# Moving the two magnitude products of the kernel tables from VectorE to GpSimd, and a longer wait for the tables' matmuls

## The chip, the cores and the metric

The kernel runs on one core of one Trainium2 chip. The metric is device time in microseconds (us) from one launch of the whole kernel. Engines are called PE (TensorE, the matmuls; PEld is its loading of weights), DVE (VectorE), ACT (ScalarE), POOL (GpSimd, which also issues some of the transfers) and SP (which issues most of the others).

## The reference

The input `x` is 2048 tokens by 576 channels, float32. It is normalised, and the result goes two ways: through a long convolution along the tokens (S4D: the convolution kernel of each channel is a sum over 128 complex exponentials), and through a two-layer MLP over the channels with 4608 hidden units.

```python
xn = layernorm(x)
# S4D: kernel K (576 x 2048), convolution by FFT
dt = exp(log_dt); A = -exp(log_A_real) + 1j*A_imag; C = (C_real + 1j*C_imag)*dt[:, None]
P = exp((A*dt[:, None])[:, :, None] * pos)          # 576 x 128 x 2048
K = 2*einsum("dn,dnl->dl", C, P).real
s = irfft(rfft(xn.T, 2L) * rfft(K, 2L))[:, :L].T + xn*D_skip
# MLP, gated
h = gelu(layernorm(xn) @ w1 + b1)
g = silu(h @ w2 + b2)
out = x + s*g
```

## The kernel before

**MLP.** The MLP sets the length of the kernel. Its products are made with operands split into a high and a low part, three matmuls for each product. Tokens are taken in 4 blocks of 512, hidden units in 12 groups of 3 x 128. One *pass* (a "slot" in the code; there are 48) is one group with one block: three times 14 matmuls of the first layer (L519, into the PSUM tiles `mxa` and `mxb`), then 72 matmuls of the second layer (L585). Between the two layers, for each of the three parts of 128 hidden units: ACT makes `h` (gelu, L552), ACT makes its high half `hh` (L555), DVE makes the low half `hl` as `h - hh` (L558). The third `hl` of a pass is needed by the 21st matmul of the second layer. DVE also adds the second layer's results into `acc` (L595) and makes the low halves of the weights (`w1l`, `w2l`, L496).

**Tables.** The convolution kernel is built from 36 tables, one for 16 channels each (`tables(b)`). The parameters `par` are loaded from memory (L810, issued by POOL, two buffers). A table's work is split into steps: phases and sines (DVE L828, L831, L837; ACT), the magnitudes `mg` (`mags`, L853: two products of broadcast parameters, of 1024 and 512 elements a partition; one buffer), and four products of sines and magnitudes (`weigh`, L864, L866, L868, L870) that give `U` and `v`. PE then makes 64 small matmuls from `U` and `v` (`kgen`, L910), which give a piece of the convolution kernel. The products `weigh` of the next table wait for these matmuls, since `U` and `v` have one buffer.

**Convolution.** Six chunks of 96 channels each go through transform steps on PE (L982, L1021, L1074, L1106), with DVE and ACT work between them. These steps use the PSUM tile `cv`.

**Order.** Each engine works through its instructions in the order in which the program is written, and a planner (class `Order`) decides that order when the kernel is built. Every step has an engine and an expected duration, for instance `dve(n)`, `act(n)` or `pool(n)` for n elements; the planner keeps a clock for each engine, sorts the steps of several *lines* into the stream, and holds back a DVE or ACT step that would delay a piece of the MLP that is due. The cost functions are

```python
def dve(n):
    return 0.075 + 0.00104 * n
...
def pool(n):
    return 0.25 + 0.0023 * n
```

The small PE steps (tables and convolution) are placed between the MLP's matmuls by `pe_turns`. A table's matmuls can go in two ways. They *ride*: when a convolution step is placed and the table is ready, `ride` puts the table's 64 matmuls at the head of that step. Or they go *alone*, but once the convolution has started only when the table has been ready for `ALONE` microseconds of planned PE time:

```python
if x is kl and pace["started"] and kl["steps"][0]["mark"][1] < NB - 1 and od.t["PE"] < h[1] + ALONE:
    break
```

Of the kernel before, what the change touches and what calls it, by code (L numbers as in the profile page):

```python
# [42 lines left out]
def dve(n):  # L43
    return 0.075 + 0.00104 * n


def act(n):
    return 0.06 + 0.00098 * n


def pool(n):
    return 0.25 + 0.0023 * n
# [155 lines left out]
def step(eng, dur, fn, need=(), mark=None, cv=0, at=0.0, late=0.0, tbl=None, by=1e9):  # L208
    return dict(eng=eng, dur=dur, fn=fn, need=tuple(need), mark=mark, cv=cv, at=at, late=late, tbl=tbl, by=by)
# [3 lines left out]
def mixer_kernel(ctx, tc, u, log_a_real, a_imag, c_real, c_imag, log_dt, d_skip, w1, b1, w2, b2,  # L213
                 f1, f2, g2, g1, tvals, ident, out, parts=("mlp", "s4d")):
    nc = tc.nc
# [589 lines left out]
    def load_par(b):  # L805
        if b == NB:
            return
        PAR[b] = sb.tile([P, SB, NPAR], F32, name="par", bufs=2)

        nc.gpsimd.dma_start(PAR[b].rearrange("p (g i) k -> p g (i k)", g=4), dram(  # L810
            par_s, (b // 6 * CH + b % 6 * 4) * NPAR, [[D * NPAR, P], [24 * NPAR, 4], [1, 4 * NPAR]]))

    def bc(ap, dim, n):

        a = [list(x) for x in ap.ap]
        a.insert(dim, [0, n])
        return bass.AP(tensor=ap.tensor, offset=ap.offset, ap=a)

    def tables(b):

        T = {}

        def phase(k):
            if k == 0:
                T["w"] = sb.tile([P, 2, SB, NV], F32, name="w", bufs=2)
                nc.vector.tensor_mul(T["w"][:, 1], bc(PAR[b][:, :, 0], 2, NV), bc(tv, 1, SB))  # L828
            else:
                u = T["w"][:, 1, :, 32:]  # L830
                nc.vector.tensor_add(u, u, bc(PAR[b][:, :, 1], 2, 32))  # L831

        def whole():
            nc.scalar.activation(T["w"][:, 0].bitcast(I32), T["w"][:, 1], AF.Copy)

        def frac():
            nc.vector.tensor_sub(T["w"][:, 1], T["w"][:, 1], T["w"][:, 0].bitcast(I32))  # L837

        def fold():
            nc.scalar.activation(T["w"][:, 0], T["w"][:, 1], AF.Abs)  # L840

        def sin(k):
            w = T["w"][:, k]
            if k == 0:
                nc.scalar.activation(w, w, AF.Sin, bias=halfpi[:, 0:1], scale=-TWO_PI)
            else:
                nc.scalar.activation(w, w, AF.Sin, scale=TWO_PI)

        def mags(k):
            if k == 0:  # L850
                T["m"] = sb.tile([P, SB, NM], F32, name="mg")
            n, e1, e8 = ((8, E1, E8), (4, E32, E256))[k]
            nc.vector.tensor_mul(T["m"][:, :, 64 * k:64 * k + 8 * n].rearrange("p c (i j) -> p c i j", i=n),  # L853
                                 bc(PAR[b][:, :, e8:e8 + n], 3, 8), bc(PAR[b][:, :, e1:e1 + 8], 2, n))

        def weigh(k, part):

            if part == 0:
                T["v"] = sb.tile([P, 2, SB, 64], F32, name="v")
                T["U"] = sb.tile([P, 2, SB, 32], F32, name="U")  # L860
                TAB[b] = (T["U"], T["v"])
            w, v, m = T["w"], T["v"], T["m"]
            if part == 0:
                nc.vector.tensor_mul(T["U"], w[:, :, :, 32:], bc(m[:, :, 64:], 1, 2))  # L864
            elif part == 1:
                nc.vector.tensor_mul(v[:, :, :, :32], w[:, :, :, :32], bc(m[:, :, :32], 1, 2))  # L866
            elif k == 0:
                nc.vector.tensor_mul(v[:, k, :, 32:], w[:, k, :, 31::-1], m[:, :, 32:64])  # L868
            else:
                nc.vector.scalar_tensor_tensor(v[:, k, :, 32:], w[:, k, :, 31::-1], -1.0, m[:, :, 32:64],  # L870
                                               op0=OP.mult, op1=OP.mult)

        n = SB * 32
        f = lambda g, *a: lambda: g(*a)
        return ([step(None, 6.0 if b < 3 else 4.5, lambda: load_par(b), mark=("par", b), need=[("pack", ((b // 6 + 1) * CH - 1) // PK)]
                      + ([("mags", b - 2)] if b > 1 else [("xn", k) for k in range(8, NT)])),
                 step("DVE", dve(SB * NV), f(phase, 0), need=[("wu", b - 2, 1)] if b > 1 else []),
                 step("DVE", dve(n), f(phase, 1)), step("ACT", act(SB * NV), whole),
                 step("DVE", dve(SB * NV), frac), step("ACT", act(SB * NV), fold, mark=("fold", b))],
                [step("ACT", act(SB * NV), f(sin, 0), need=[("fold", b)], mark=("sin", b, 0), tbl="sin"),  # L880
                 step("ACT", act(SB * NV), f(sin, 1), mark=("sin", b, 1), tbl="sin")],
                [step("DVE", dve(2 * n), f(mags, 0), need=[("par", b)]),
                 step("DVE", dve(n), f(mags, 1), mark=("mags", b))]
                + [step("DVE", dve(2 * n) if part < 2 else dve(n), f(weigh, k, part),
                        need=[("sin", b, int(part < 2))] + ([("kg", b - 1)] if b else []),
                        mark=("wu", b, 1) if k else None) for k, part in ((0, 0), (0, 1), (0, 2), (1, 2))])
# [491 lines left out]
    def wmark(n, which):  # L1378

        per = KB + 1 + G  # L1380
        a = n * per + (0 if which == 1 else KB + 1)
        return [("w", k) for k in range(a, a + (KB + 1 if which == 1 else G))]
# [21 lines left out]
    for k in range(4):  # L1404
        gl["steps"].append(step("POOL", 5.0, lambda k=k: part.update({k: load_g2(k)}), mark=("g2", k),
                                need=[("g2c", k - 1)] if k else []))
# [10 lines left out]
    def table_lines():  # L1417
        for b in range(NB):
            for x, y in zip((tl, sl, vl), tables(b)):
                x["steps"] += y  # L1420
            kl["steps"] += kgen(b)
# [21 lines left out]

    pace = dict(left=NCH * (2 + 2 + 4), last=0.0, started=False)
    END = 960.0
    ALONE = 7.0

    def pe_turns(limit=1, any_time=False, all_lines=True):
        for x in (nl, pl, ml) + ((c3, c1, kl) if all_lines else ()):
            n = 0  # L1450
            while n < (2 if x in (c1, nl) else limit):
# [3 lines left out]
                if x is c1:  # L1455
# [5 lines left out]
                    pace["left"] -= 1  # L1461
                if x is kl and pace["started"] and kl["steps"][0]["mark"][1] < NB - 1 and od.t["PE"] < h[1] + ALONE:
                    break
# [22 lines left out]
    def l2_terms(k):  # L1486

        if k < 4:
            a = [(i, dh) for dh in range(2) for i in range(G - 1)]
            b = [(G - 1, dh) for dh in range(2)]  # L1490
            return ((0, a, False, range(G - 1)), (1, a[:2], False, range(G - 1)),
                    (0, b, True, (G - 1,)), (1, a[2:] + b, True, range(G)))[k]
        j, dh = k // 2, k % 2
        return j, [(i, dh) for i in range(G)], dh == 1, range(G)
# [38 lines left out]
    for slot in range(NSLOT):  # L1533
        turn[0] = slot + 1
        n, g, tb = SEQ[slot]
        change = slot + 1 < NSLOT and SEQ[slot + 1][0] != n
        final = slot >= NSLOT - 2
        for pos in range(NPOS):
            if pos < G:
                need = wmark(n, 1) + [("x", tb)]  # L1540
# [24 lines left out]
            else:  # L1565
                j, terms, last, hid = l2_terms(pos - G)
                need = [wmark(n, 2)[i] for i in hid] + [("h", slot, i) for i in hid]
# [15 lines left out]
                if last or halves:  # L1583
                    add = cell[0]
                    dh, k = (terms[0][1], 1) if halves else (0, 2)
# [5 lines left out]
                    if final:  # L1591
                        b = 8 + 4 * tb + j
# [72 lines left out]
```

## Time and profile before

| what | value |
|---|---|
| median of 3 runs | 1073.8 us (1073.32 to 1075.48) |
| the profiled execution's own time | 1074.78 us |
| its span, first to last instruction | 1073.0 us |
| granted PE clock | 0.999 |
| PE busy | 1065.7 us, 99% of the span |
| DVE busy | 952.1 us, 89% |
| ACT busy | 693.3 us, 65% |
| POOL busy | 206.8 us, 19% |
| the two products L853 on DVE | 72 instructions, 155.5 to 919.2 us |

How to read it: a group's row gives the line, the engine, the operation, the tile written and the tiles read, the shapes and the number of instructions; then the busy time in us, the mean duration of one in ns, and the time for which the engine stood idle just before them, with what ended it. A row of the timeline gives start and duration in us. A row of the waits gives the total in us, the number of waits, and the longest. The ends of matmuls are modelled by the profiler, so their starts are the better measure.

### The profile page before, as it was taken

Reading aid. Unit: us, or ns where it says so; the run is one execution under the profiler, and the core shown is the slowest. Engines: PE = TensorE matmul, PEld = TensorE weight load, DVE = VectorE, ACT = ScalarE, POOL = GpSimd, SP = SyncE. Lnnn points to the kernel's source line nnn. Section 1 sums busy time; section 2 is a strip of 40 time slices with the busy share of each in tenths; the row PEclk is TensorE's granted clock in tenths of the full one; section 3 lists DMA queues with packets and bytes.
Section 4 is the critical chain, followed back from the end, with each engine's and each line's share of the span. In section 5 each row is a group of like instructions: output and inputs, shape, how many; then the busy total and the mean of one; then the engine's idle time right before and its main releaser. Section 6 shows DMA issues by size and latency. Waiting matters only on the chain.

```text
span 1073.0 us, 25798 instructions
## 1 busy us (share of the span) xinstructions
PE 1065.7 (99%) x10703; PEld 926.8 (86%) x10703; DVE 952.1 (89%) x1530; ACT 693.3 (65%) x1063; POOL 206.8 (19%) x294
## 2 busy tenths in 40 slices
PE   9999999999999999999999999999999999999998
PEld 7989999888888888888888888788887888888887
DVE  7789968989898999999999989999999999866657
ACT  6656768867657586686866667667585676525353
POOL 6669433111000001100120000200011022322020
PEclk9999999999999999999999999999999999999999
DMA  7885455654223332356322233232431437454146
GB/s 230 240 257 194 130 194 197 209 116 130 74 66 106 50 90 73 108 142 145 89 73 77 68 75 97 50 99 64 87 97 43 132 100 167 123 185 135 38 117 168
DMA packets 139573, 129.62 MB, mean 121 GB/s; under 512 B 89628, under 2 KB 111296, under 8 KB 138432
## 3 DMA queue, kind: packets, MB, share of 16 engines
q1 hardware_dynamic: 122944, 78.31, 27.3%
q0 software_dynamic: 15760, 48.70, 15.0%
q8 instruction: 84, 1.38, 0.6%
q10 hardware_dynamic: 752, 0.97, 0.3%
q14 instruction: 33, 0.27, 0.1%
HBM read 98.50 MB, written 35.19 MB: 125 GB/s over the span
## 4 chain that ended last, share of the span: by engine, by line
PE 96%; DVE 2%; DMA 0%; ACT 0%; issue 0%; ACTq 0%; DVEq 0%
PE mxa L519 21%; PE mxb L585 21%; PE mxb L519 21%; PE mxa L585 21%; PE cv L910 3%; PE cv L1021 3%; PE cv L982 2%; PE cv L1074 2%; PE cv L1106 1%; DMA acc<-in_A_u_dram 0%; PE cv L585 0%; PE mxa L534 0%; DVE pr L749 0%; DVE row L394 0%; DVE acc L595 0%
## 5 line engine op out<-in xcount | busy, mean ns | idle before, releaser
L585 PE MATMUL mxb<-w2h,hh 128*128 128x288 f32 x573 | 170.2, 297 | 0.0
L585 PE MATMUL mxb<-w2h,hl 128*128 128x288 f32 x573 | 169.6, 296 | 0.0
L585 PE MATMUL mxb<-w2l,hh 128*128 128x288 f32 x573 | 168.6, 294 | 0.0
L585 PE MATMUL mxa<-w2h,hh 128*128 128x288 f32 x567 | 168.5, 297 | 0.0
L585 PE MATMUL mxa<-w2h,hl 128*128 128x288 f32 x567 | 167.9, 296 | 0.2 <-DVE hl L558 0.2
L585 PE MATMUL mxa<-w2l,hh 128*128 128x288 f32 x567 | 166.8, 294 | 0.0
L558 DVE TENSOR_TENSOR hl<-h,hh 128x512 fp32r<-128x512 f32 x144 | 99.3, 691 | 67.8 <-ACT hh L555 67.2
L810 POOL DMA_DIRECT2D par<-par_s x36 | 27.5, 764 | 463.9 <-DVE mg L853 412.2
L552 ACT ACTIVATE h<-mxa,b1t 128x512 f32<-128x512 f32 x73 | 50.1, 688 | 101.7 <-PE mxa L519 97.8
L585 PEld LDWEIGHTS mxb<-w2h,hh 128*128 128x128 f32 x573 | 107.6, 188 | 6.9 <-issue 3.0
L585 PEld LDWEIGHTS mxa<-w2h,hh 128*128 128x128 f32 x567 | 106.5, 188 | 7.4 <-issue 5.3
L585 PEld LDWEIGHTS mxb<-w2l,hh 128*128 128x128 f32 x573 | 107.6, 188 | 0.7
L585 PEld LDWEIGHTS mxb<-w2h,hl 128*128 128x128 f32 x573 | 107.5, 188 | 0.6 <-DVE hl L558 0.3
L585 PEld LDWEIGHTS mxa<-w2h,hl 128*128 128x128 f32 x567 | 106.4, 188 | 0.9 <-DVE hl L558 0.8
L585 PEld LDWEIGHTS mxa<-w2l,hh 128*128 128x128 f32 x567 | 106.5, 188 | 0.7
L552 ACT ACTIVATE h<-mxb,b1t 128x512 f32<-128x512 f32 x71 | 48.9, 689 | 74.8 <-PE mxb L519 71.1
L555 ACT ACTIVATE hh<-h 128x512 fp32r<-128x512 f32 x144 | 90.8, 632 | 4.1
L499 ACT ACTIVATE w2h<-raw 128x576 fp32r<-128x576 f32 x75 | 46.5, 675 | 56.5 <-PE mxa L585 53.5
L519 PE MATMUL mxa<-XH,w1h 128*128 128x512 f32 x284 | 78.7, 399 | 0.0
L519 PE MATMUL mxb<-XH,w1h 128*128 128x512 f32 x280 | 78.1, 401 | 0.0
L519 PE MATMUL mxa<-XL,w1h 128*128 128x512 f32 x284 | 76.2, 390 | 0.0
L519 PE MATMUL mxa<-XH,w1l 128*128 128x512 f32 x284 | 76.0, 389 | 0.0
(251 smaller groups left out, 2497.5 us busy)
## 6 DMA issues: line engine op xcount, KB each, us to landing
raw<-in_B_w_dram SPq DMA_DIRECT2D x75, 288.0 KB, 3.1
raw<-in_B_w_dram SPq DMA_DIRECT2D x100, 192.0 KB, 3.2
par_s<-A POOLq DMA_DIRECT2D x8, 1080.0 KB, 6.0
par<-par_s POOLq DMA_DIRECT2D x36, 240.0 KB, 3.3
f2t<-f2q SPq DMA_DIRECT2D x24, 256.0 KB, 3.3
raw<-in_B_w_dram SPq DMA_DIRECT2D x50, 96.0 KB, 3.6
u_s<-in_A_u_dram POOLq DMA_DIRECT2D x16, 288.0 KB, 4.5
xc<-xn_s SPq DMA_DIRECT2D x48, 96.0 KB, 3.7
```

The lines of the kernel that those rows point to most:

```text
L499: nc.scalar.activation(h, r, AF.Copy)
L519: nc.tensor.matmul(q, a, b, start=j == 0, stop=j == len(ops) - 1)
L552: nc.scalar.activation(t, q, AF.Gelu_apprx_tanh, bias=b1t[:, g * G + i:g * G + i + 1], scale=1.0)
L555: LAST[0] = nc.scalar.activation(hh[:, i], t, AF.Copy)
L558: nc.vector.tensor_sub(hl[:, i], t, hh[:, i].bitcast(F32))
L585: nc.tensor.matmul(q[:, dh, :288], a[:, i, c], b[:, i, d], start=i == 0 and k == 0 and not alone, stop=i == G - 1 and k == 2, skip_group_c ...
L810: nc.gpsimd.dma_start(PAR[b].rearrange("p (g i) k -> p g (i k)", g=4), dram(par_s, (b // 6 * CH + b % 6 * 4) * NPAR, [[D * NPAR, P], [24 * ...
L910: nc.tensor.matmul(q[32 * g:32 * g + 32, i // 2, i % 2 * 64:i % 2 * 64 + 64], U[:, ri, 4 * g + i, :], v[:, ri, 4 * g + i, :], start=ri == ...
L982: nc.tensor.matmul(Q1ST[i, x][g // 2][64 * f:64 * f + 64, g % 2].rearrange(order), f1t[r].rearrange("p s k -> p (s k)"), rhs(r, f), start= ...
L1021: nc.tensor.matmul(Q[i][32 * q:32 * q + 32, f, 2 * ri:2 * ri + 2], m[r, 4 * i + q, 32 * ri:32 * ri + 32], A2[r, 4 * p + 2 * i + q // 2, :, ...
L1074: nc.tensor.matmul(QI[q // 2][64 * h:64 * h + 64, q % 2, i], MAT["g2t", p + h][r, i, ri], YS[p + h][0][r, i, ri], start=ri == 0, stop=ri == 1,
L1106: nc.tensor.matmul(Q[f][32 * e:32 * e + 32, t], g1t[r], A2[r, k:k + 2, 1].rearrange("p i d r -> p i r d"), start=True, stop=True, skip_gro ...
```

## The change

The two products of `mags` are issued on POOL instead of DVE, and the planner books them on POOL with POOL's cost function. A table's matmuls go alone after 9 us of waiting for a convolution step, not after 7.

```diff
@@ mags(k)
             n, e1, e8 = ((8, E1, E8), (4, E32, E256))[k]
-            nc.vector.tensor_mul(T["m"][:, :, 64 * k:64 * k + 8 * n].rearrange("p c (i j) -> p c i j", i=n),
+            nc.gpsimd.tensor_mul(T["m"][:, :, 64 * k:64 * k + 8 * n].rearrange("p c (i j) -> p c i j", i=n),
                                  bc(PAR[b][:, :, e8:e8 + n], 3, 8), bc(PAR[b][:, :, e1:e1 + 8], 2, n))
@@ the steps of a table
-                [step("DVE", dve(2 * n), f(mags, 0), need=[("par", b)]),
-                 step("DVE", dve(n), f(mags, 1), mark=("mags", b))]
+                [step("POOL", pool(2 * n), f(mags, 0), need=[("par", b)]),
+                 step("POOL", pool(n), f(mags, 1), mark=("mags", b))]
@@ the pacing of PE's small steps
-    ALONE = 7.0
+    ALONE = 9.0
```

## The prediction

> **What bounds the kernel now.** I read the page's busy times and its chain first, then the three stretches before, during and after the tables, then TensorE's waits.
>
> ```profile
> span 1073.0 us, 25798 instructions
> PE 1065.7 (99%) x10703; PEld 926.8 (86%) x10703; DVE 952.1 (89%) x1530; ACT 693.3 (65%) x1063; POOL 206.8 (19%) x294
> PE 96%; DVE 2%; DMA 0%; ACT 0%; issue 0%; ACTq 0%; DVEq 0%
> ```
> ```profile
> core 0: us, PE busy (x) PEld busy (x) DVE busy (x) ACT busy (x) POOL busy (x), PEclk, DMA share, GB/s
> 155.00:925.00 770.00, 769.99 (x8522) 666.26 (x8521) 726.19 (x1124) 535.57 (x800) 82.67 (x135) 1.00 0.37 101
> ```
> ```profile
> PE cv L421 <- DVE row L394: 0.3, 1, 0.3
> PE mxa L585 <- DVE hl L558: 0.2, 1, 0.2
> ```
>
> TensorE is the bound: 96% of the chain. All 72 products that move run between 155 and 920 us, and in that stretch TensorE is busy 769.99 of 770 us at full clock. VectorE's 89% looks like a second bound, but over the whole span TensorE waited for it 0.5 us in all. So an easier VectorE has almost nothing to give; only what makes TensorE wait, or changes its own work, moves the time.
>
> Matmul ends are modelled, so short waits hide in "busy" and must be read from the starts. The tightest place is the third low half `hl` of a pass, made by VectorE just before TensorE needs it. Here are the first and the last of the tight ones in the stretch, `hl` and then the matmuls around its use:
>
> ```profile
> 158.96 0.68 DVE L558 TENSOR_TENSOR hl<-h,hh 128x512 fp32r<-128x512 f32 x1
> ...
> 159.55 0.29 PE L585 MATMUL mxb<-w2l,hh 128*128 128x288 f32 x1
> 159.69 0.40 PE L585 MATMUL mxb<-w2h,hl 128*128 128x288 f32 x1
> 159.93 0.29 PE L585 MATMUL mxb<-w2h,hh 128*128 128x288 f32 x1
> ```
> ```profile
> 882.21 0.69 DVE L558 TENSOR_TENSOR hl<-h,hh 128x512 fp32r<-128x512 f32 x1
> ...
> 883.27 0.29 PE L585 MATMUL mxb<-w2h,hl 128*128 128x288 f32 x1
> ```
>
> The first ends at 159.64 and is used at 159.69: no room, and the next matmul starts 0.24 us later instead of the usual 0.13. The last ends at 882.90 and is used at 883.27: 0.36 us of room. Of the 34 passes in the stretch, 19 have 0.36 us or less (6 of them 0.13 or less).
>
> **The change, part by part.**
>
> *VectorE loses the two products.*
>
> ```profile
> L853 DVE TENSOR_TENSOR mg<-par 128x1024 f32<-128x1024 f32 x36 | 43.9, 1220 | 0.6
> L853 DVE TENSOR_TENSOR mg<-par 128x512 f32<-128x512 f32 x36 | 24.6, 684 | 0.0
> ```
>
> That is 36 x (1.220 + 0.684) = 68.5 us, 1.9 us a table. None of it is on the chain. What it can give is the late `hl` of the six tightest passes, about 0.1 us each as at 159.93, so at most 0.7 us; I take 0, because the next part makes `hl` late again.
>
> *GpSimd gains them.* No row shows this product there; the nearest rows bound it:
>
> ```profile
> L496 POOL TENSOR_TENSOR w1l<-raw,w1h 128x384 fp32r<-128x384 f32 x2 | 2.0, 1014 | 0.0
> L403 POOL TENSOR_SCALAR A<-A,U 128x576 f32<-128x576 f32 x4 | 9.8, 2449 | 0.1
> ```
>
> The two-input product there takes 1014/384 = 2.64 ns an element, the one-input pass 2449/576 = 4.25. So the larger product costs 2.7 to 4.4 us and the smaller 1.35 to 2.2; I take the low ends, since it is the same operation: 4.05 us a table, 146 us in all. GpSimd is busy 82.67 of 770 us in the stretch, so 229 of 770 afterwards; the room hides it. The planner books 2.6 and 1.4 us, which fits. At the high ends, 6.6 us a table, the products that use `mg` would come 2.6 us later than planned (a rival below).
>
> *GpSimd's queue.* The products issue no transfer, but the queue is in order, and a product must wait for its parameters and for the one `mg` buffer, which VectorE frees with L870 of the table before.
>
> ```profile
> POOL par L810 <- DVE mg L853: 412.2, 26, 33.2
> POOL s_s L1117 <- ACT pr L1114: 94.4, 6, 41.4
> ```
>
> The parameter load already waits for `mg` (412 us in 26 waits), so that wait turns into the queue's own order. Behind a product now stand parameter loads, the stores of a chunk's result, and the combine's loads and stores. Each may come some 4 us later; their users are a table or a chunk away (770/36 = 21 us, or over 100), so I take 0. If that cover were gone, a late load would cost its 4 us once.
>
> *VectorE and GpSimd side by side.* This is the part that decides. The trace shows GpSimd's one-input passes beside VectorE's `hl`, which has two inputs in on-chip memory:
>
> ```profile
> 24.15 0.96 DVE L558 TENSOR_TENSOR hl<-h,hh 128x512 fp32r<-128x512 f32 x1 [0.31 <-ACT hh L555]
> ...
> 23.74 2.29 POOL L403 TENSOR_SCALAR acc<-acc,U 128x576 f32<-128x576 f32 x1
> ```
> ```profile
> 59.17 0.93 DVE L558 TENSOR_TENSOR hl<-h,hh 128x512 fp32r<-128x512 f32 x1 [1.55 <-ACT hh L555]
> 62.34 1.01 DVE L558 TENSOR_TENSOR hl<-h,hh 128x512 fp32r<-128x512 f32 x1 [0.67 <-ACT hh L555]
> ...
> 58.73 2.29 POOL L403 TENSOR_SCALAR A<-A,U 128x576 f32<-128x576 f32 x1
> 61.98 2.29 POOL L403 TENSOR_SCALAR A<-A,U 128x576 f32<-128x576 f32 x1
> ```
>
> These three take 0.93 to 1.01 us instead of 0.69, and all end 1.37 us after the GpSimd pass began. So each moved only from 1.37 - 0.69 = 0.68 us after that start: 0.68/576 = 1.2 ns for each element that GpSimd reads. Conversely, in one place GpSimd was held:
>
> ```profile
> 54.05 1.62 DVE L496 TENSOR_TENSOR w2l<-raw,w2h 128x576 fp32r<-128x576 f32 x2
> ...
> 54.86 2.88 POOL L403 TENSOR_SCALAR A<-A,U 128x576 f32<-128x576 f32 x1
> ```
>
> (2.88 us instead of 2.29, until the `w2l` ended.) What a two-input GpSimd product does to VectorE no row shows. The low end is the 0.3 us of these rows. The high end is the whole product, 2.7 and 1.35 us. I take two reads an element at 1.2 ns, near the high end, as two inputs are the case: 2 x 1024 x 1.2 = 2.4 us and 1.2 us.
>
> A good half of VectorE's work in the stretch reads two operands from on-chip memory (`hl`, `w1l`, `w2l`, the rest of the tables). Its instructions last 726/1124 = 0.65 us, so I let the first that is caught come 0.7 us after a product starts. Then each table holds VectorE up by (2.4 - 0.7) + (1.2 - 0.7) = 2.2 us, more than the 1.9 us it saves. The saving is in the planner's books; the hold is not.
>
> A late VectorE recovers only in its idle time: (770 - 726.2 + 68.5)/770 = 0.146 us per us. So 2.2 us last 15 us of the 21 that a table takes: VectorE is late 0.7 of the time, by 1.1 us on average. In half of the tight passes I let idle time ahead of `hl` swallow it, as before the `hl` at 59.17. That leaves 19 x 0.7 x 0.5 = 6.7 stalls of 1.1 - 0.36 = 0.74 us: +4.9 us. Above: without swallowing, twice that, +9.8; below: a hold of 0.3 us fits into the 0.36, so 0.
>
> *The longer wait for a convolution step.* A table's 64 matmuls (L910) either go between the main matmuls alone or ride ahead of a convolution step:
>
> ```profile
> 266.33 0.29 PE L585 MATMUL mxa<-w2h,hl 128*128 128x288 f32 x1
> 266.55 1.10 PE L910 MATMUL cv<-v,U 128*32 128x64 f32 x64
> 267.58 0.40 PE L585 MATMUL mxb<-w2h,hh 128*128 128x288 f32 x1
> 267.81 0.29 PE L585 MATMUL mxb<-w2l,hh 128*128 128x288 f32 x1
> ...
> 793.29 1.10 PE L910 MATMUL cv<-v,U 128*32 128x64 f32 x64
> ```
>
> Alone it costs 0.22 + 0.24 us at the borders instead of 0.13 twice: 0.2 us. Riding, those borders are paid by the step anyway. After the convolution has begun 5 of the 36 went alone (first and last shown). Waiting 9 instead of 7 us can spare at most 5 x 0.2 = 1.0 us, and nothing if no step comes in the added 2 us; I take two, -0.4.
>
> *Sum.* 1074.8 (the profiled execution: span 1073.0 and 1.8 around it) + 4.9 - 0.4 = 1079.3. That execution was 1.0 us above the median of 1073.8, so the forecast is 1078.3, +0.4%.
>
> **The rivals.**
>
> *No hold worth the name (not slower).* If a caught instruction loses 0.3 us as in the rows, 72 x 0.3 = 22 us against 68.5 saved, VectorE is easier throughout, and no `hl` passes its 0.36. It decides as soon as the hold stays under about 0.5 us a product. For it: the only rows there are. Against: they are one-input passes. Time: 1073.8 - 0.4 = 1073.4, and 1072.1 with all rides (-1.0) and the 0.7.
>
> *The whole product holds VectorE, and nothing swallows it.* (2.7 - 0.7) + (1.35 - 0.7) = 2.65 us a table lasts 18 of 21 us; 19 x 0.85 x (1.33 - 0.36) = 15.6: 1089. Against: `hl` was free at 0.68 of 2.29 us. The Trainium skill ("SBUF — State Buffer", "Who interferes with whom") says that a VectorE instruction with two SBUF inputs and a GpSimd instruction that reads SBUF exclude each other, the loser blocked for the whole instruction; by it this rival's sum holds. The trace agrees on the blocking (0.93 to 1.01 us for 0.69) and not on the whole instruction.
>
> *GpSimd slow at the products themselves.* At 4.25 ns an element `mg` comes 2.6 us late, VectorE stands at the product L864, and the same 2.2-us reasoning gives about +6: 1079. Against: the operation's own row at 2.64.
>
> *Faster after all.* All five rides, the 0.7 us, and one wait more must come together: 1071.5.
>
> **How the numbers follow.** Forecast 0.42, no hold 0.36, whole hold 0.08, slow products 0.06, faster 0.08. The range goes from the no-hold case with all its gains, 1072.2, to 1086, beyond the unswallowed 1083 and short of most of the 1089. The forecast's own is 1075.5 to 1083. About 0.2%, 2.1 us, is what a measurement here can tell from no change. Slower: 0.42 + 0.08 + 0.06, less the forecast's lowest part, 0.54. Same: 0.38. Faster: 0.08.
>
> **What would show it.** `mg` on POOL x72 near 2.7 and 1.35 us; VectorE's busy time down less than 68.5 us, its two-input instructions in the stretch with maxima of 2 us and more; TensorE waiting for `hl` (L558) in five to ten places; L910 alone fewer than five times after the first step. The forecast is wrong if `hl` keeps near 0.69 us throughout, or if it is held and TensorE's waits stay under 1 us.

## The result and the profile after

The change made the kernel slower: 1102.8 us (median; 1102.4 to 1104.0) against 1073.6, a ratio of 1.027 (95% interval 1.0252 to 1.0288), 29 us. The forecast was 1078.3 with a range up to 1086. The direction was right, the size far off.

The page's span and busy times, and the stretch of the tables:

```profile
span 1102.1 us, 25859 instructions
PE 1074.5 (97%) x10703; PEld 930.6 (84%) x10703; DVE 955.7 (87%) x1458; ACT 683.3 (62%) x1055; POOL 349.7 (32%) x366
```
```profile
core 0: us, PE busy (x) PEld busy (x) DVE busy (x) ACT busy (x) POOL busy (x), PEclk, DMA share, GB/s
155.00:925.00 770.00, 750.46 (x8344) 645.69 (x8343) 718.10 (x1034) 516.18 (x779) 219.92 (x195) 1.00 0.36 97
```

TensorE makes the same 10703 matmuls, but in the stretch where it was busy 769.99 of 770 us it now stands still for 19.5 us. (The granted clock of the stretch rounds to 1.00 before and after; two short places below full clock come below.) VectorE lost its 72 products and is busy *longer* than before (955.7 us against 952.1). The groups show where that time is: VectorE's `hl`, before and then after, and GpSimd's products:

```profile
L558 DVE TENSOR_TENSOR hl<-h,hh 128x512 fp32r<-128x512 f32 x144 | 99.3, 691 | 67.8 <-ACT hh L555 67.2
L558 DVE TENSOR_TENSOR hl<-h,hh 128x512 fp32r<-128x512 f32 x144 | 118.8, 828 | 60.4 <-ACT hh L555 60.0
```
```profile
L853 POOL TENSOR_TENSOR mg<-par 128x1024 f32<-128x1024 f32 x36 | 90.2, 2507 | 428.1 <-DVE v L870 407.0 <-issue 21.0
L853 POOL TENSOR_TENSOR mg<-par 128x512 f32<-128x512 f32 x36 | 54.3, 1509 | 0.0
```

`hl` grew from 99.3 us in all to 118.8. The instructions by line, with minimum, median and maximum of one in ns, say how. Here are `hl` and the addition to `acc`, which reads one operand from PSUM (TensorE's result memory) and one from SBUF (the on-chip memory), first before and then after:

```profile
L558 DVE TENSOR_TENSOR hl<-h,hh x144: 626/686/1015, 21.5 to 1059.8; 128x512 fp32r<-128x512 f32 x144
L595 DVE TENSOR_TENSOR acc<-mxb,acc x86: 705/751/758, 45.3 to 1050.4; 128x576 f32<-128x576 f32 x86
```
```profile
L558 DVE TENSOR_TENSOR hl<-h,hh x144: 627/691/2461, 21.7 to 1088.9; 128x512 fp32r<-128x512 f32 x144
L595 DVE TENSOR_TENSOR acc<-mxb,acc x86: 703/751/758, 45.5 to 1078.1; 128x576 f32<-128x576 f32 x86
```

The median of `hl` hardly moved (686 and 691 ns) and its maximum went from 1.02 to 2.46 us: some are held, most are not. `acc`, with its one operand in PSUM, is never held. TensorE's waits name the things that come late:

```profile
PE mxb L585 <- DVE hl L558: 6.2, 7, 1.5
PE mxa L585 <- DVE hl L558: 5.3, 6, 1.5
PE mxb L585 <- DVE acc L595: 4.1, 5, 2.3
PE mxa L585 <- DVE acc L595: 4.0, 3, 2.4
PE mxa L585 <- ACT h L552: 0.7, 1, 0.7
```

That is 19.6 us in 21 waits for VectorE, and 0.7 us in one for ACT. The view shows each wait too short, since the ends of matmuls are modelled: at the wait below it says 1.50 us, while the matmul starts 533.24 - 531.45 = 1.79 us after the one before it instead of 0.13, and the next one 0.24 later instead of 0.13. So 1.66 + 0.11 - 1.50 = 0.27 us are missing; for all 22 waits that makes about 6 us (an estimate from this one).

About 3 us more are TensorE's clock. In two places of the stretch it was granted half its clock (0.50), for 3.4 us each; before, no place of the stretch was below full clock. The rows have the columns of the stretch above, with PEclk third from the end:

```profile
160.30:163.70 3.40, 3.37 (x14) 3.38 (x15) 3.10 (x5) 3.38 (x7) 0.00 (x0) 0.50 0.00 0
392.40:395.80 3.40, 3.40 (x17) 3.40 (x16) 2.36 (x5) 0.96 (x2) 0.00 (x0) 0.50 0.72 273
```

There the matmuls of L585 start 0.24 us apart instead of 0.13, which costs about 2 x 3.4 x (1 - 0.13/0.24) = 3.1 us (an estimate). Both places begin within 1.2 us of the end of a wait of TensorE (1.05 us at 160.3, 2.33 us at 391.2), but the longest wait, 2.39 us at 318.4, is followed by none. What lowers the clock stays open. Together, 19.6 + 0.7 + 6 + 3 us account for the 29.

Here is one of the waits, from the timelines of GpSimd, VectorE and TensorE:

```profile
528.16 4.47 POOL L853 TENSOR_TENSOR mg<-par 128x1024 f32<-128x1024 f32 x2 [32.21 <-DVE v L870]
```
```profile
527.39 0.69 DVE L870 SCALAR_TENSOR_TENSOR v<-w,mg 128x512 f32<-128x512 f32 x1
528.11 1.23 DVE L828 TENSOR_TENSOR w<-par,tv 128x1024 f32<-128x1024 f32 x1
529.37 2.34 DVE L831 TENSOR_TENSOR w<-w,par 128x512 f32<-128x512 f32 x1
531.64 1.55 DVE L558 TENSOR_TENSOR hl<-h,hh 128x512 fp32r<-128x512 f32 x1
```
```profile
531.45 0.29 PE L585 MATMUL mxb<-w2l,hh 128*128 128x288 f32 x1
533.24 0.40 PE L585 MATMUL mxb<-w2h,hl 128*128 128x288 f32 x1 [1.50 <-DVE hl L558]
533.48 0.29 PE L585 MATMUL mxb<-w2h,hh 128*128 128x288 f32 x1
```

GpSimd had waited 32 us for L870, which frees `mg`, and began at the very moment when VectorE went on to the next table. L828 was running and takes its usual 1.2 us; the first product waits for it (a product that meets nothing takes 1.97 us, this one 3.0). L831 follows and is held by the product, 2.34 us instead of 0.69; then `hl` by the second product, 1.55 instead of 0.69. The pair of products ends at 532.63 and `hl` at 533.19, 0.56 us later: the hold lasted to the product's end. The other held `hl` and L831 end 0.55 or 0.56 us behind a product too, with few exceptions. TensorE gets this `hl` 1.66 us late.

### The profile page after: what moved, and what is told of

Same layout as the page of the kernel before. It is cut to its first block, busy times and chain, and to the rows that moved or that the text cites. A ratio compares the mean times of both kernels' runs of the same rounds, so it can differ in the third digit from the quotient of the medians.

```text
span 1102.1 us, 25859 instructions
## 1 busy us (share of the span) xinstructions
PE 1074.5 (97%) x10703; PEld 930.6 (84%) x10703; DVE 955.7 (87%) x1458; ACT 683.3 (62%) x1055; POOL 349.7 (32%) x366
## 5 line engine op out<-in xcount | busy, mean ns | idle before, releaser
L853 POOL TENSOR_TENSOR mg<-par 128x1024 f32<-128x1024 f32 x72 | 143.3, 2008 | 428.2 <-DVE v L870 407.0
L585 PE MATMUL mxb<-w2h,hl 128*128 128x288 f32 x573 | 171.2, 299 | 6.3 <-DVE hl L558 6.2
L585 PE MATMUL mxb<-w2h,hh 128*128 128x288 f32 x573 | 171.4, 299 | 4.1 <-DVE acc L595 4.1
L585 PE MATMUL mxa<-w2h,hh 128*128 128x288 f32 x567 | 169.9, 300 | 4.8 <-DVE acc L595 4.0
L585 PE MATMUL mxa<-w2h,hl 128*128 128x288 f32 x567 | 168.8, 298 | 5.3 <-DVE hl L558 5.3
L558 DVE TENSOR_TENSOR hl<-h,hh 128x512 fp32r<-128x512 f32 x144 | 118.8, 828 | 60.4 <-ACT hh L555 60.0
L585 PE MATMUL mxb<-w2l,hh 128*128 128x288 f32 x573 | 169.4, 296 | 0.0
L585 PE MATMUL mxa<-w2l,hh 128*128 128x288 f32 x567 | 167.3, 295 | 0.0
L585 PEld LDWEIGHTS mxa<-w2h,hh 128*128 128x128 f32 x567 | 107.0, 189 | 15.3 <-DVE acc L595 6.6
L585 PEld LDWEIGHTS mxb<-w2h,hh 128*128 128x128 f32 x573 | 108.4, 189 | 11.6 <-DVE acc L595 5.8
L585 PEld LDWEIGHTS mxb<-w2h,hl 128*128 128x128 f32 x573 | 108.3, 189 | 8.4 <-DVE hl L558 8.3
L585 PEld LDWEIGHTS mxa<-w2h,hl 128*128 128x128 f32 x567 | 106.8, 188 | 7.3 <-DVE hl L558 7.2
L585 PEld LDWEIGHTS mxb<-w2l,hh 128*128 128x128 f32 x573 | 108.3, 189 | 0.6
L585 PEld LDWEIGHTS mxa<-w2l,hh 128*128 128x128 f32 x567 | 107.0, 189 | 0.6
L595 DVE TENSOR_TENSOR acc<-mxa,acc 128x576 f32<-128x576 f32 x86 | 64.2, 746 | 23.1 <-PE mxa L585 23.0
L595 DVE TENSOR_TENSOR acc<-mxb,acc 128x576 f32<-128x576 f32 x86 | 64.4, 749 | 15.2 <-PE mxb L585 15.1
```

The costliest lines, as they stand in the source:

```text
L558: nc.vector.tensor_sub(hl[:, i], t, hh[:, i].bitcast(F32))
L585: nc.tensor.matmul(q[:, dh, :288], a[:, i, c], b[:, i, d], start=i == 0 and k == 0 and not alone, stop=i == G - 1 and k == 2, skip_group_c ...
L595: nc.vector.tensor_add(o, q[:, dh:dh + n, :288], b if first else o)
L853: nc.gpsimd.tensor_mul(T["m"][:, :, 64 * k:64 * k + 8 * n].rearrange("p c (i j) -> p c i j", i=n), bc(PAR[b][:, :, e8:e8 + n], 3, 8), bc(P ...
```

## The experiments

Each kernel ran beside the kernel before. "Held" is VectorE's busy time above the 893.6 us of e4, the run in which GpSimd reads nothing. In e5, e10 and e12 VectorE's own work differs from that of e4. There "held" is the sum of the durations of VectorE's instructions above e4's 983.4 us, less the product that stays on VectorE (24.6 us in e5, 43.9 in e10) or plus the step left out (43.7 in e12); busy time counts the overlap of neighbouring records once, so durations can't be taken from it. (By durations the change has 63 us.) "Lost" is the median against that of before. In the cuts of code below, `[...]` stands for what is left out, and what follows `#` is a remark.

| run | time, us | ratio (95%) | held, us | lost, us |
|---|---|---|---|---|
| the change | 1102.8 | 1.027 (1.0252 to 1.0288) | 62 | 29.1 |
| e4: GpSimd only writes | 1074.4 | 1.000 (0.9991 to 1.0009) | 0 | 0.0 |
| e3: plan of before | 1094.9 | 1.0191 (1.0176 to 1.0207) | 65 | 20.5 |
| e2: wait of 7 us | 1107.6 | 1.0312 (1.0288 to 1.0337) | 58 | 33.2 |
| e5: larger product only, wait of 7 us | 1094.7 | 1.0188 (1.0171 to 1.0205) | 46 | 20.4 |
| e6: products in pieces | 1095.4 | 1.0199 (1.0184 to 1.0214) | 41 | 21.0 |
| e7: products twice | 1178.1 | 1.0969 (1.0933 to 1.1006) | 136 | 103.8 |
| e8: one operand | 1079.7 | 1.005 (1.0035 to 1.0065) | 25 | 5.4 |
| e10: smaller product only, plan of before | 1078.9 | 1.0045 (1.0028 to 1.0062) | 19 | 4.6 |
| e12: more room on VectorE | 1096.0 | 1.0197 (1.0182 to 1.0213) | 64 | 21.5 |
| e13: VectorE, not booked | 1087.6 | 1.0119 (1.0102 to 1.0136) | no product | 13.2 |
| e11: GpSimd only writes, wait of 7 us | 1076.3 | 1.0017 (1.0008 to 1.0026) | 0 | 1.8 |

**Is it the hold? (e4)** The order of the change, but GpSimd writes constants instead of multiplying.

```diff
-            nc.gpsimd.tensor_mul(T["m"][...], bc(PAR[b][...]), bc(PAR[b][...]))
+            for _ in range(3):
+                nc.gpsimd.memset(T["m"][:, :, 64 * k:64 * k + 8 * n], 0.001)
```

> The order of the changed kernel is kept, but GpSimd fills mg with a constant in three passes instead of multiplying: it writes and reads nothing (the magnitudes are left out, the parameters are not read). The three passes should take about 3.1 and 1.6 us, at least as long as the products (2.5 and 1.5 us). Theory hold (a GpSimd product that reads keeps VectorE's two-input instructions waiting, 66 us in all): VectorE's hl falls back from 828 to about 690 ns, the waits of TensorE for hl and acc vanish, and the time is 1073 to 1075 us. Rival order (the plan with the products booked on GpSimd puts hl and acc too late by itself): about 1095 to 1103 us, waits as before. Rival late mg (the products end too late for the table's other products): also 1100 or more.

```profile
L854 POOL MEMSET mg<- 128x1024 f32 x108 | 103.3, 957 | 405.8 <-DVE v L870 401.7
L854 POOL MEMSET mg<- 128x512 f32 x108 | 56.7, 525 | 4.1
```
```profile
155.00:925.00 770.00, 770.00 (x8632) 664.62 (x8632) 674.27 (x1067) 524.22 (x792) 243.10 (x357) 1.00 0.38 105
```

GpSimd is busy even longer in the stretch than with the products (243.1 us against 219.9), at the same places, and the whole loss is gone: TensorE is busy 770 of 770 us again. So the new order costs nothing; what GpSimd *reads* does. Nor does a late `mg`: VectorE waits for it 2.6 us in two waits here, and not at all in the change. The run also shows the other half: VectorE's busy time is 58.5 us below that of before (893.6 against 952.1; the products' 68.5 us are durations, which overlap their neighbours), and the time is that of before within 0.1%. The Trainium skill ("SBUF — State Buffer", "Who interferes with whom") says that a VectorE instruction with two SBUF inputs contends with a GpSimd instruction that reads SBUF, not with one that only writes. The runs agree: 62 us held with the products, none with the constants (here no L831 lasts over 0.70 us and in the tables' stretch no `hl` over 0.72, against 3.60 and 2.46 in the change), and `acc` with its one SBUF input never held.

**Hold or plan? (e3)** The kernel before, its plan included; only the engine of the two products differs.

```diff
-            nc.vector.tensor_mul(T["m"][...], ...)
+            nc.gpsimd.tensor_mul(T["m"][...], ...)     # still booked as DVE steps, ALONE = 7.0
```

> The kernel before with nothing changed but the engine of the two products: the planner still books 1.9 us a table for them on VectorE and TensorE's order is that of before, convolution steps included. Theory hold: the holds are about the same, 1.8 us a table, but the books keep 1.9 us of VectorE's time free for them; stalls come only from where a hold falls just ahead of an hl or acc, so 1078 to 1092 us. If the hold costs the same wherever VectorE has room: 1100 us. Rival order (the new plan and not the hold is to blame): 1073 to 1075 us.

```profile
L853 POOL TENSOR_TENSOR mg<-par 128x1024 f32<-128x1024 f32 x36 | 76.8, 2134 | 393.7 <-DVE v L870 393.5
PE mxa L585 <- DVE acc L595: 3.3, 2, 1.7
PE mxb L585 <- DVE hl L558: 2.8, 5, 1.0
PE mxa L585 <- DVE hl L558: 2.5, 3, 1.5
```

1094.9 us, a little above the 1078 to 1092 expected. TensorE's order and VectorE's booked time are those of the kernel before. The plan keeps free 58.5 us of VectorE's busy time (what e4 lost with the products), nine tenths of the 65 us of holds, and still 20.5 us are lost. Booking the time doesn't cure it.

**The time or its place? (e13, e12)** e13 is the mirror image: the products on VectorE, booked on GpSimd, in the order of the change. e12 keeps the change and leaves out VectorE's fractional part of the phase, which stays booked.

```diff
e13 -            nc.gpsimd.tensor_mul(T["m"][...], ...)
    +            nc.vector.tensor_mul(T["m"][...], ...)     # still booked as POOL steps
e12 -            nc.vector.tensor_sub(T["w"][:, 1], T["w"][:, 1], T["w"][:, 0].bitcast(I32))
    +            pass
```

> The changed kernel's order, with the two products issued on VectorE after all, while the planner still books them on GpSimd: 1.9 us a table of VectorE's time that the plan doesn't know, about as much as the holds, and no GpSimd product. Theory room (any unbooked VectorE time of this size makes hl and acc late, whatever it comes from): 1090 to 1105 us. Theory place (a hold is worse than the same time, since it falls on the two-input instruction that runs beside the product, hl above all): 1075 to 1085 us.

> The changed kernel with one of VectorE's table steps left out but still booked (the fractional part of the phase, L837, 1.21 us a table, 44 us): the order is the same and VectorE has 1.2 us a table more room than the plan knows. Theory room: about two thirds of the holds are paid by it, and the loss falls from 29 to 5 to 12 us: 1079 to 1086. Theory place (holds hit hl and acc directly, and room elsewhere doesn't help): 1095 to 1102 us.

```profile
L558 DVE TENSOR_TENSOR hl<-h,hh 128x512 fp32r<-128x512 f32 x144 | 98.9, 688 | 59.6 <-ACT hh L555 59.2
L853 DVE TENSOR_TENSOR mg<-par 128x1024 f32<-128x1024 f32 x72 | 68.4, 949 | 0.3
```

(e13's rows.) Neither theory alone holds. 57 us of unbooked VectorE busy time (950.7 us against e4's 893.6), with no `hl` held, lose 13.2 us, between the two expectations: less than half of the 29. And 44 us of extra room take 7.6 us off the loss, leaving 21.5 (1096.0 us): far from "room", and at the low end of "place". The room gave a little more than that: e12's profiled execution has 13.6 us at half clock against the change's 6.8, some 2 us of extra loss (an estimate). So e12 speaks for the place of a hold, and e13 says that unbooked time costs something too. By these runs unbooked time alone costs 13, holds in a plan that keeps most of the time free cost 20, and both together 29.

**How the loss grows (e5, e10, e8, e7, e6).** Less of the products, one operand instead of two, each product twice, each in four pieces:

```diff
e5  +            (nc.vector if k else nc.gpsimd).tensor_mul(...)   # larger one on POOL and booked there, ALONE = 7.0
e10 +            (nc.gpsimd if k else nc.vector).tensor_mul(...)   # smaller one on POOL, plan of before
e8  +            nc.gpsimd.tensor_copy(T["m"][...], bc(PAR[b][:, :, e8:e8 + n], 3, 8))
e7  +            for _ in range(2): nc.gpsimd.tensor_mul(...)
e6  +            for c in range(0, SB, 4): nc.gpsimd.tensor_mul(T["m"][:, c:c + 4, ...], ...)
```

> Only the larger product goes to GpSimd and is booked there, the smaller stays on VectorE; wait of 7 us. Theory hold: holds of up to 1.9 us by 36 products instead of 72, some 40 us of the 66; stalls fall about in proportion or somewhat more, 1085 to 1095 us. Rival (it is the pair in a row that hurts, a single product is absorbed): 1074 to 1078 us. Rival order: still about 1095 to 1103 us.

> The kernel before with only the smaller product on GpSimd and the plan of before. Theory hold: 36 holds of at most 1.1 us, 15 to 25 us in all; at 0.3 us lost for each us held 1078 to 1082 us. If a hold under the 1.2 us that lie ahead of many an hl is absorbed: 1073 to 1076 us.

> The changed kernel with a copy of one broadcast operand in place of each product (the second factor is left out): GpSimd reads one operand instead of two. By the prediction's own reading (1.2 ns an element read) a hold ends 1.2 and 0.6 us after the copy begins, the holds shrink to about half, 25 to 40 us, and the time to 1083 to 1090 us. If the whole copy holds VectorE, the hold ends with the copy. If one operand does not hold VectorE: 1073 to 1075 us.

> The changed kernel with both products made twice on GpSimd (same values, booked once). Theory hold: the holds double, some 130 us, and the stalls follow with 0.3 to 0.45 us for each us held, as in the runs so far (66 us held, 20 to 29 us lost; 47 us held, 20 lost): 1115 to 1135 us. If stalls saturate because TensorE's waits give VectorE its room back: 1105 to 1112 us.

> The changed kernel with each product cut into four pieces of 256 or 128 elements (eight GpSimd instructions a table instead of two, same values). Theory A, a VectorE instruction with two operands in on-chip memory waits for the end of the GpSimd instruction that runs: no single wait above 0.6 us instead of 1.9, the two engines take turns, hl never above 1.4 us; the sum of the holds stays at 50 to 100 us, and the time at 1085 to 1105. If single long holds make the stalls: 1074 to 1082 us. Theory B, the engines share a bandwidth and VectorE slows down in proportion to what GpSimd reads: the same as the changed kernel, 1098 to 1106 us, and lengthened instructions throughout.

GpSimd's rows in e8 and e6, and `hl` in e6:

```profile
L853 POOL COPY mg<-par 128x1024 f32<-128x1024 f32 x36 | 56.5, 1568 | 454.9 <-DVE v L870 433.7 <-issue 21.1
L853 POOL COPY mg<-par 128x512 f32<-128x512 f32 x36 | 36.4, 1011 | 0.0
```
```profile
L855 POOL TENSOR_TENSOR mg<-par 128x256 f32<-128x256 f32 x144 | 138.9, 993 | 369.0 <-DVE v L872 351.2 <-issue 17.7
L558 DVE TENSOR_TENSOR hl<-h,hh x144: 626/693/1419, 21.4 to 1080.3; 128x512 fp32r<-128x512 f32 x144
```

In the plan of the change the loss grows faster than the hold: 25 us held lose 5 (e8, 0.2 for each), 41 lose 21 (e6, 0.5), 62 lose 29 (the change, 0.5), 136 lose 104 (e7, 0.8). e10 and e5, in other plans, agree (19 lose 5, 46 lose 20), so a single product a table hurts too and it does not take the pair. So small holds are partly absorbed, and e7 came out well above the 1115 to 1135 expected from a constant rate. Some of that is the clock: e7's mean granted clock over its span is 0.983 against 0.999 before, about 0.016 x 1173.5 = 19 of its 104 us (an estimate), which leaves 0.6 for each us held. e8 shows that one operand suffices to hold (25 us), and less time is held, as the copies are shorter (1.04 and 0.62 us unhindered); a held `hl` ends 0.54 us behind the copy, so here too the whole instruction holds; it lost less than the 9 to 16 us expected. In e6 the longest `hl` is 1.42 us instead of 2.46, so a hold ends with one GpSimd instruction and not with the whole of GpSimd's reading. But the engines then take turns up to eight times a table, and 21 us are lost, not the 0 to 8 of "single long holds".

**The wait for a step (e2, e11).** Both put the wait back to 7 us, e2 in the change, e11 in e4.

```diff
-    ALONE = 9.0
+    ALONE = 7.0
```

> The changed kernel with the old wait of 7 us for a convolution step. Theory hold: the wait for a step is worth under 1 us, so 1098 to 1106 us, moved only by where the holds happen to fall. Rival (the longer wait is what costs: a table's matmuls come later, and the rest with them): 1074 to 1085 us.

> The run with GpSimd only writing constants into mg (the magnitudes are left out), with the old wait of 7 us for a convolution step: what the longer wait is worth where no hold is. Prediction's step: 0.2 us for each table that rides instead of going alone, so at most 1 us: 1073.5 to 1075.5 us. Rival (the longer wait costs or saves more by itself): outside 1072 to 1077.

Without holds the longer wait gives 1074.4 against 1076.3 us. The intervals of the two ratios touch (0.9991 to 1.0009, 1.0008 to 1.0026), and the two did not run side by side, so about 2 us is an indication, more than the 1 us allowed for. After the first convolution step, TensorE's timelines have 4 tables alone in e4 and in the change, 7 in e11 and e2, and 5 before. So in the new plan the longer wait spares three tables, at some 0.6 us each; the change against before spares one. With holds, 7 us gives 33 us lost instead of 29 (1107.6 us, just above the 1098 to 1106 expected). The longer wait is not the cause of the slowdown; it hid a part of it.

## Why the prediction was wrong

**Right.** TensorE bounds the kernel, and an easier VectorE gives nothing (e4: 0.0 us). The products on GpSimd fit into its idle time, and its queue, late parameters and late stores cost nothing (e4 again, with GpSimd busier still). The decisive part is the hold between the two engines. Its sum was near: forecast 36 x 2.2 = 79 us, measured 62. "More than it saves" came true, by little: without the products VectorE's busy time fell by 58.5 us (e4), the holds put 62 back, and it rose by 3.6 us. The 68.5 us of the forecast are durations, which overlap; the idle time that makes up lateness is (770 - 674.27)/770 = 0.124 us per us by e4, not 0.146.

**A near sum by luck, from two wrong parts.** The product's low end, 2.7 and 1.35 us, was still high: unhindered it takes 1.97 and 1.07. And a hold does not end after 1.2 ns for each element read, a rate from one-input passes that took 2.29 us and held for 0.68; it ends with the product. The two errors cancel (2.4 and 1.2 us assumed, 1.97 and 1.07 measured). The rival "the whole product holds VectorE" had the better mechanism, and the rule of the Trainium skill behind it ("SBUF — State Buffer", "SBUF: two separate sides": whichever starts first keeps the port for the whole instruction, and the other is blocked) is what the trace of after shows for these products: the held `hl` above ends 0.56 us behind the product. Its 1089 was still too low, since it goes through the same conversion into stalls.

**The step that failed** is the conversion of lateness into stalls: "6.7 stalls of 0.74 us: +4.9". Measured are 21 waits for `hl` and `acc`, of 0.93 us on average by the view, and 29 us in all. The prediction

- counted only the third `hl` of tight passes. 8 of the 21 waits, 8.1 us, are for `acc`, which is never held itself but comes late when instructions ahead of it were held;
- treated lateness as spread evenly, 1.1 us on average, of which idle time swallows half. e13 has that kind of lateness, 1.9 us a table with no hold, and lost 13.2 us, with 10 waits for `hl` and 6 for `acc`: averaging and the missing `acc` together were low by more than half;
- left out the place. The product starts right behind L870, and what runs beside it is then often L831 or `hl` itself, held for up to 1.8 us where there is 0.36 us of room. e3, in which the plan keeps most of the time free, lost 20.5 us;
- had no term for TensorE's clock, about 3 us here.

The range was built from the same conversion ("without swallowing, twice that"), so it failed with it. How much of the gap each of these points makes up, no run separates. The wait of 9 us was forecast to let two more tables ride than before; one more did. e11 and e4 put the worth of 9 against 7 us in the new plan nearer to 2 us than to 0.4, as an indication.

No run beat the kernel before. Where the holds vanish the time is that of before, since TensorE has no wait left to give up.

## What to carry to other kernels

Before moving a product from VectorE to GpSimd, count what VectorE has beside it: where its instructions read two operands from on-chip memory, GpSimd's reading stopped them here, and the time moved came back as delay at a place that no plan knew. In this kernel, whose matmul engine is full, a freed engine was worth nothing, and a single delay came through as a wait of up to 2.4 us. When you turn delays into stalls, take the delay where it falls and every consumer behind it, not an average over the period.

## What the runs showed of the hardware

- GpSimd's two-input product of 128x1024 took 1.97 us unhindered, against VectorE's 1.22; its one-input pass (L403) took 2.29 us for 576 elements and held VectorE for only 0.68 us of them. Why that pass releases VectorE early was not tried.
- Both wait for each other: a product that began while VectorE's L828 was under way took 3.0 us, 1.0 more than unhindered.
- Filling `mg` three times (0.96 and 0.53 us a pass) held VectorE not at all.
- Runs with many stalls have places of 3.4 or 6.8 us in which TensorE was granted half its clock (two in the change, 6.8 us in all). Before, e4, e8 and e10 have none in the tables' stretch, but neither have e5 and e13, which lost 20 and 13 us.
